# Four engines in written order across the hand-over between two stages, and low parts moved to GpSimd, in a gated attention and feed-forward kernel

## The chip, the cores and the metric

The kernel runs on one core of a Trainium2 chip. A core has a matrix engine (TensorE, PE in the profile), whose weight loads are listed apart (PEld), a vector engine (VectorE, DVE), a scalar engine (ScalarE, ACT), a general engine (GpSimd, POOL) and a queue that issues transfers (SyncE, SP). Each works through its own list of instructions in the order in which the list was built, and waits for the others through semaphores. The metric is the time of one execution on the device in microseconds (us); less is better.

## The reference, cut to what matters

```python
x = A_x                                            # 2048 tokens x 576, float32
g = sigmoid((x * gate_w).sum(-1, keepdims=True))   # one gate for each token
# A: linear attention, 32 heads of 18
q, k, v = heads(x @ wqkv)
pq, pk = q @ w_phi, k @ w_phi                      # by head
phi_q = [softmax(pq), softmax(-pq)]                # 36 features, phi_k likewise
kv, z = phi_k^T v, sum of phi_k over the tokens
a = (phi_q kv) / (phi_q z + 1e-6) @ wo
# B: feed-forward, 576 -> 4608 -> 576
gate, up = x @ W_gate, x @ W_up
b = (relu(gate) * up) @ W_down
out = g * a + (1 - g) * b
```

## The kernel before, in words

All products are to have float32 accuracy. An operand is split into a high part in the matrix engine's reduced format and a low part, the rest: ScalarE rounds a copy (the high part), another engine subtracts it from the source (the low part), and a product takes three passes: high by high, high by low, low by high. Every operand that enters a product therefore costs a copy on ScalarE and a subtraction, and the matmul waits for whichever part comes last.

**Attention, first half (to about 260 us).** Tokens are taken in 16 tiles of 128, four tiles to a block of 512. `load_x` loads a block's tokens (two transfers into tiles `xr` of the 4-buffer pool `raw`) and splits them into `xh`, `xl` and `x4`; `x4` holds the last 64 rows' high part and, in its other half, their low part. Block 0 is made ahead of the loop; the loop `for t in range(2, NT - 2)` makes block 1 at t = 3, block 2 at t = 6 and block 3 at t = 10. In a step t the matrix engine projects keys (`pk`), values (`kv`) and queries (`pq`) of a tile from `xh`, `xl`, `x4`, adds to the sums over keys (`kv<-e,vt`) and turns features (`ptr<-ident,e`). VectorE finds maxima and minima, subtracts them, sums the exponentials (`sm`) and scales one half of the features; GpSimd scales the others (L209, `e<-e,sm` for a key tile, `e<-e,r` for a query tile). PE, DVE and ACT are ordered here by the scheduler, GpSimd alone by `in_order`.

**Attention, second half.** The queries stand in four blocks of 512, b = 0 to 3. `sums(b, ..)` multiplies features by `kv`; `invert` and `split_inverse` make the reciprocals `rd`; `divide(b, k)` spreads `rd` over a bank (PE, L624), multiplies it into `R` (DVE, L626), copies the high part `oh` (ACT, L627) and subtracts the low part `ol` (DVE, L628). `project_out(b, m)` multiplies the five pieces k by `wo` for the output rows m, into one bank out of four (pool `pv1`, called `pw`, and `kv_bank(0..2)`, called `kv`), each of them one buffer: for b = 2, m = 0, 2, 4 take `pw` and m = 1, 3 take `kv2`; for b = 3, m = 0 to 4 take `kv1`, `pw`, `kv2`, `kv0`, `kv1`. So (2,4) may start when the copy of (2,2) has left `pw`, and (3,1) when (2,4) has left it. `rows_out` takes a bank out: for m < 4 one copy by ACT (L780), for m = 4 a copy by ACT (L782) and an addition by DVE that reads the bank too (L783).

**Hand-over to the feed-forward part.** Its products combine blocks of weights and of tokens (seven products `cx`, `ca`, `cy` in place of eight, L1122). Needed for the first of them are seven combined token operands `xo` and weights `wb` and `ws` for the first two groups of columns. Operands 0 to 2 are loaded ahead into `xr` and split by `operand_ahead`, a generator: its first step is the high part (ACT, L811), its second the low part (DVE, L815 and L825). Operands 3 to 6 are loaded in place and split by `in_place` (ACT L840 and L841, DVE L845 and L825). `first_weights` is a generator of steps: high parts of `wb` (ACT, L858), low parts (DVE, L861 and L864), four block sums in the raw weights `wr` (DVE, L879 to L882), and the same split for `ws`, which reads the sums. It also calls `in_place`.

From the end of the first half on, `in_order(tc, nc, nc.tensor, nc.sync, nc.gpsimd)` ties PE, SP and GpSimd to the order in which the code is written. ACT and DVE are not tied: the scheduler picks for them, except that `behind()` keeps the pieces of operands and weights behind the last instruction written before them and behind each other. A piece inside `behind()` may thus come much later than where it is written, behind the copies and divisions that are written after it. The names `first_out`, `root_rows`, `fetch` and `gather` are other steps of the attention part and stay as they are.

After this comes the feed-forward part, which is most of the time: `cx`, `ca`, `cy` products, ACT copies `g` and `u` out of their banks (L1288), DVE combinations (L1407 to L1412), and the down projection.

Of the kernel before, what the change touches and what calls it, by code (L numbers as in the profile page):

```python
# [7 lines left out]
F32 = mybir.dt.float32  # L8
# [7 lines left out]
P = 128  # L16
# [67 lines left out]
def gated_mix_kernel(  # L84
# [59 lines left out]
    wv_l = ka.tile([P, 5, VP], F32R, name="wv_l")  # L144
    bd = raw.tile([FG, NF, FG], F32, name="bd", tag="raw")

    def split(hi, lo, src):
        nc.scalar.activation(hi, src, AF.Copy)
        tt(out=lo, in0=src, in1=hi.bitcast(F32), op=SUB)

    X = {}

# [2 lines left out]
                 xp.tile([P, TB], F32R, name="x4"))  # L155
        return X[tb]

    def split_x4(x4, src):
        nc.scalar.activation(x4, src, AF.Copy)
        tt(out=x4[64:], in0=src[64:], in1=x4[64:].bitcast(F32), op=SUB)  # L160
# [12 lines left out]
    def accumulate(ps, pairs):  # L173
        for i, (w, m) in enumerate(pairs):
# [122 lines left out]
    def whole(steps):  # L297
        for _ in steps:
            pass
# [604 lines left out]
    def low_parts(f, u):  # L904
        f(u, low_w)
        f(u, low_w_rows)

    def first_weights():
        with behind():
            blocks(0, high_w)  # L910
            low_parts(blocks, 0)
            sums_of_blocks(0)
        yield
        with behind():
            blocks(1, high_w)
# [12 lines left out]
        yield  # L928
        for i in range(4, 7):
            in_place(i)  # L930
            yield
# [19 lines left out]
            load_operand(0, 2, nc.gpsimd)  # L951

    def in_place(i):
        with behind():
            high_in_place(0, i)
            low_in_place(0, i)
            low_rest(0, i, tt)

    with in_order(tc, nc, nc.tensor, nc.sync, nc.gpsimd):
        x0, x1, x2 = (operand_ahead(i) for i in range(3))  # L960
# [24 lines left out]
        for m in range(5):  # L985
            project_out(1, m)
            if m < 3:
                two = pp.tile([P, 2, TB], F32, name="po", tag="pp")
                sums(3, ORDER[2 * m:2 * m + 2], (two[:, 0], two[:, 1]))
            if m == 2:  # L990
                gather(3, 4)
            if m > 0:
                for k in ((), (4,), (3,), (2, 1), (0,))[m]:
                    divide(2, k)
            if m in (0, 1):
                root_rows(m + 2)
            if m == 2:
                with after(tc, nc, nc.vector, last_of(nc, nc.vector)):
                    invert(3)
                gather(3, 3, 2, 1, 0)  # L1000
                whole(split_inverse(3))
                whole(x0)
        for m in range(5):
            project_out(2, m)
            if m == 0:
                divide(3, 4)
                divide(3, 3)
                whole(x1)
            if m == 1:
                weights = first_weights()  # L1010
                for k in (2, 1, 0):
                    divide(3, k)
                RS.close()
                pad = ctx.enter_context(tc.tile_pool(name="pad2", bufs=1, **R_))
                pad.tile([P, 24], F32, name="pad2")
                xo2 = ctx.enter_context(tc.tile_pool(name="xo2", bufs=4, **R_))
                wop = ctx.enter_context(tc.tile_pool(name="wop", bufs=2, **R_))
                wraw = ctx.enter_context(tc.tile_pool(name="wraw", bufs=2, **R_))
                load_w(0)
                load_in_place(0, 3)  # L1020
                load_rests(0, (3, 4, 5))
                load_w(1)
                for i in range(4, 7):
                    load_in_place(0, i)
                whole(x2)
                load_rests(0, (6,))
                load_down(0)
                next(weights)
            if m > 1:
                next(weights)  # L1030
        load_w(2)
        for m in range(5):
            project_out(3, m)
            if m < 3:
                next(weights)
    AP.close()
    BS.close()

# [588 lines left out]
```

## Time and profile before

| what | value |
| --- | --- |
| three runs | 1592.48, 1590.77, 1590.91 us; median 1590.91 us |
| profiled execution | 1590.56 us |
| its span in the trace | 1588.8 us |
| PE busy | 1570.9 us (99% of the span) |
| DVE busy | 1190.6 us (75%) |
| ACT busy | 559.1 us (35%) |
| POOL busy | 175.0 us (11%) |
| mean granted TensorE clock | 0.999 |

The profile is one execution. A row of the timeline reads: start in us, duration in us, engine, line of the kernel, operation, output <- inputs with their shape, count of merged instructions, and in brackets the engine's idle time just before it with the instruction that ended it. Rows of waits read: waiting engine and line <- engine and line that released it: total us, number of times, longest us. Rows of windows read: stretch in us, its length, then busy us and count for PE, PEld, DVE, ACT, POOL, then the granted clock of PE as a fraction of full speed, the DMA engines' busy share and GB/s. The times are from the start of the span. Tile names have lost their numbers in these rows: `pw`, `kv` stand for the banks, `o` for the output rows, `R`, `oh`, `ol` for pieces of the divisions.

### The profile page before, as it was taken

How to read it: one execution, taken by the hardware profiler on the slowest of the kernel's cores; microseconds unless marked ns; L12 is line 12 of the kernel's file. 1: busy time of each engine (PE TensorE's matmuls, PEld its weight loads, DVE VectorE, ACT ScalarE, POOL GpSimd, SP SyncE). 2: the span in 40 equal slices, each digit the busy share in tenths (PEclk: the TensorE clock that was granted, in tenths of full speed). 3: DMA queues.
4: the chain of work that ended last, by engine and by line, in shares of the span. 5: the costliest groups of instructions: out<-in, count | busy, mean ns of one | idle time of the engine just before them, and what ended most of it. 6: DMA issues, size and time to landing. Idle time of an engine off the chain costs nothing.

```text
span 1588.8 us, 20172 instructions
## 1 busy us (share of the span) xinstructions
PE 1570.9 (99%) x7823; PEld 1312.6 (83%) x7823; DVE 1190.6 (75%) x1865; ACT 559.1 (35%) x918; POOL 175.0 (11%) x243
## 2 busy tenths in 40 slices
PE   9999999999999999999999999999999999999998
PEld 9999995577888888888888888888888888888887
DVE  4997775577778877787777777777777777777777
ACT  4444335553323333332333234232233232222321
POOL 0125521110000000000000002111111111111110
PEclk9999999999999999999999999999999999999999
DMA  5365415587655576555554516543343343443432
GB/s 171 108 205 182 154 41 158 162 331 283 217 213 210 215 257 221 215 198 216 198 195 179 208 77 229 193 172 148 140 180 146 143 177 131 167 168 131 179 140 75
DMA packets 64539, 283.38 MB, mean 178 GB/s; under 512 B 6802, under 2 KB 17298, under 8 KB 55740
## 3 DMA queue, kind: packets, MB, share of 16 engines
q1 hardware_dynamic: 61228, 270.34, 46.8%
q0 software_dynamic: 2352, 10.11, 2.0%
q10 hardware_dynamic: 864, 1.65, 0.3%
q8 instruction: 61, 1.00, 0.3%
q14 instruction: 34, 0.28, 0.0%
HBM read 172.07 MB, written 108.60 MB: 177 GB/s over the span
## 4 chain that ended last, share of the span: by engine, by line
PE 94%; DVE 4%; ACT 1%; DMA 0%; issue 0%; POOL 0%; SPq 0%; ACTq 0%; DVEq 0%; POOLq 0%
PE cx L1122 29%; PE ca L1122 14%; PE pd L1162 12%; PE pd L1185 10%; PE cy L1122 7%; PE kv L175 4%; PE pk L175 3%; PE pq L175 3%; PE pm L1162 2%; PE pm L1185 2%; PE kv L416 1%; PE ptr L374 1%; PE po L556 1%; PE pv L237 1%; PE pw L175 1%; PE psf L259 1%
## 5 line engine op out<-in xcount | busy, mean ns | idle before, releaser
L1227 ACT ACTIVATE hh<-g 128x512 fp32r<-128x512 f32 x195 | 119.9, 624 | 457.2 <-DVE g L1284 287.8
L1200 DVE TENSOR_TENSOR ac<-pd,ac 128x512 f32<-128x512 f32 x238 | 163.9, 689 | 144.4 <-PE pd L1185 144.2
L1122 PE MATMUL cx<-xo,ws 128*128 128x512 f32 x1008 | 253.5, 391 | 3.3 <-ACT g L1288 3.3
L1122 PE MATMUL ca<-xo,ws 128*128 128x512 f32 x1008 | 251.9, 389 | 0.0
L1122 PE MATMUL cx<-xo,wb 128*128 128x512 f32 x1008 | 249.1, 389 | 1.5 <-DVE u L1409 1.5
L1122 PEld LDWEIGHTS cx<-xo,ws 128*128 128x128 f32 x1008 | 190.0, 189 | 43.2 <-ACT g L1288 3.7
L1122 PEld LDWEIGHTS cx<-xo,wb 128*128 128x128 f32 x1008 | 188.1, 188 | 42.5 <-DVE u L1409 1.9
L1122 PEld LDWEIGHTS ca<-xo,ws 128*128 128x128 f32 x1008 | 189.2, 188 | 39.3
L1162 PE MATMUL pd<-hh,wd 128*128 128x512 f32 x576 | 200.7, 389 | 0.0
L1185 PE MATMUL pd<-hh,wd 128*128 128x512 f32 x476 | 185.2, 389 | 0.0
L1168 DVE TENSOR_TENSOR ac<-pd,ac 128x512 f32<-128x512 f32 x144 | 99.0, 688 | 105.3 <-PE pd L1162 102.5
L1232 DVE TENSOR_TENSOR hl<-g,hh 128x512 fp32r<-128x512 f32 x195 | 135.3, 694 | 1.9 <-ACT hh L1227 0.2
L1288 ACT ACTIVATE g<-cx 128x512 f32<-128x512 f32 x144 | 84.7, 588 | 130.1 <-PE cx L1122 130.0
L1162 PEld LDWEIGHTS pd<-hh,wd 128*128 128x128 f32 x576 | 108.1, 188 | 22.6
L1122 PE MATMUL cy<-xo,wb 128*128 128x512 f32 x504 | 126.0, 389 | 0.0
L1085 ACT ACTIVATE wd<-wdr 128x384 fp32r<-128x384 f32 (+1 forms) x106 | 62.3, 607 | 144.5 <-DMA wdr<-wd 144.5
L1162 PE MATMUL pd<-hl,wd 128*128 128x512 f32 x288 | 112.0, 389 | 0.0
L1122 PEld LDWEIGHTS cy<-xo,wb 128*128 128x128 f32 x504 | 94.8, 188 | 19.8
L1185 PEld LDWEIGHTS pd<-hh,wd 128*128 128x128 f32 x476 | 89.4, 188 | 18.5
L1185 PE MATMUL pd<-hl,wd 128*128 128x512 f32 x238 | 92.6, 389 | 0.0
L825 POOL TENSOR_TENSOR xo<-xr,xo 32x512 fp32r<-32x512 f32 x5 | 8.3, 1668 | 614.6 <-ACT xo L841 614.6
L1088 DVE TENSOR_TENSOR wd<-wdr,wd 128x384 fp32r<-128x384 f32 (+1 forms) x106 | 68.8, 663 | 2.0 <-ACT wd L1085 2.0
(256 smaller groups left out, 2559.8 us busy)
## 6 DMA issues: line engine op xcount, KB each, us to landing
wsd<-ws SPq DMA_DIRECT2D x34, 1280.0 KB
ws<-wsd SPq DMA_DIRECT2D x34, 1280.0 KB
wbd<-wb SPq DMA_DIRECT2D x34, 960.0 KB
wb<-wbd SPq DMA_DIRECT2D x34, 960.0 KB
wr<-wgu SPq DMA_DIRECT2D x36, 768.0 KB
wdr<-wd SPq DMA_DIRECT2D x36, 576.0 KB
eT<-et SPq DMA_DIRECT2D x10, 594.0 KB
xt<-xb SPq DMA_DIRECT2D x7, 768.0 KB
```

Source lines behind the costliest of these rows:

```text
L175: nc.tensor.matmul(ps, w, m, start=i == 0, stop=i == len(pairs) - 1)
L237: nc.tensor.matmul(pv[i][c], m, w_[:, k, cs], start=k == 0 and n == 0, stop=k == 4 and n == 1)
L1085: nc.scalar.activation(o[:, 0], a, AF.Copy)
L1088: tt(out=o[:, 1], in0=a, in1=o[:, 0].bitcast(F32), op=SUB)
L1122: nc.tensor.matmul(ps, w, v, start=first and m == 0, stop=m == len(pairs) - 1, skip_group_check=True)
L1162: nc.tensor.matmul(ps, w, v, start=k == 0 and (i < 2 or first), stop=k == len(mms) - 1 and (i < 2 or last), skip_group_check=True)
L1168: tt(out=a, in0=ps, in1=a, op=ADD)
L1185: mm = lambda ps, w, v, a, z: nc.tensor.matmul(ps, w, v, start=a, stop=z, skip_group_check=True)
L1200: tt(out=a, in0=ps, in1=a, op=ADD)
L1227: nc.scalar.activation(h, src, AF.Copy)
L1232: tt(out=l, in0=src, in1=h.bitcast(F32), op=SUB)
L1288: nc.scalar.activation(a, ps, AF.Copy)
```

## The change

Three things are done.

First, block 1's tokens. `load_x` becomes a generator that issues both loads and then, in a second step, splits. For block 1 the loads are issued at t = 2 and the split is written at t = 3 as before, with `pt`, GpSimd's subtraction, in place of DVE's. With it the first three pieces are copied and subtracted one at a time (128x512 each) instead of as one 128x1536 instruction.

Second, operand 0's split (`x0`) is written after the step m = 4 of the loop over `project_out(1, m)`, behind the divisions of block 2, where it stood at m = 2.

Third, the hand-over. From `project_out(2, 1)` on, `in_order` holds all engines, DVE and ACT included, and `behind()` is taken out of `first_weights` and `in_place`. The transfers are written as `load_w(0)`, `load_w(1)`, the four in-place loads, three of the rests, `load_down(0)`; operand 2's split and the last rest move into `first_weights`, into its third step; `load_w(2)` moves behind the last `project_out`.

```diff
-    def load_x(tb):
+    def load_x(tb, f=tt):
         s = slice(tb * TB, (tb + 1) * TB)
         xh, xl, x4 = x_tiles(tb)
-        a = raw.tile([P, 3, TB], F32, name="xr", tag="raw")
+        a, b = (raw.tile([P, n, TB], F32, name="xr", tag="raw") for n in (3, 2))
         nc.sync.dma_start(a, xT[:, 0:3, s])
-        split(xh[:, 0:3], xl[:, 0:3], a)
-        b = raw.tile([P, 2, TB], F32, name="xr", tag="raw")
         nc.sync.dma_start(b, xT[:, 3:5, s])
-        split(xh[:, 3], xl[:, 3], b[:, 0])
-        split_x4(x4, b[:, 1])
+        yield
+        for k in (slice(0, 3),) if f is tt else range(3):
+            split(xh[:, k], xl[:, k], a[:, k], f)
+        split(xh[:, 3], xl[:, 3], b[:, 0], f)
+        split_x4(x4, b[:, 1], f)
...
-            if t in (3, 6, 10):
-                load_x((t + 2) // 4)
+            if t == 2:
+                second = load_x(1, pt)
+                next(second)
+            if t == 3:
+                whole(second)
+            if t in (6, 10):
+                whole(load_x(t // 4 + 1))
...
     def first_weights():
-        with behind():
-            blocks(0, high_w)
-            low_parts(blocks, 0)
-            sums_of_blocks(0)
+        blocks(0, high_w)
+        low_parts(blocks, 0)
+        sums_of_blocks(0)
         yield
-        with behind():
-            blocks(1, high_w)
-            low_parts(blocks, 1)
+        blocks(1, high_w)
+        low_parts(blocks, 1)
         yield
-        with behind():
-            block_sums(0, high_w)
-            sums_of_blocks(1)
-        with behind():
-            block_sums(1, high_w)
-            low_parts(block_sums, 0)
+        block_sums(0, high_w)
+        whole(x2)
+        load_rests(0, (6,))
+        sums_of_blocks(1)
+        yield
+        low_parts(block_sums, 0)
+        block_sums(1, high_w)
         yield
         in_place(3)
-        with behind():
-            low_parts(block_sums, 1)
+        low_parts(block_sums, 1)
         yield
...
                 whole(split_inverse(3))
+            if m == 4:
                 whole(x0)
-        for m in range(5):
+        project_out(2, 0)
+        divide(3, 4)
+        divide(3, 3)
+        whole(x1)
+    with in_order(tc, nc, nc.tensor, nc.vector, nc.scalar, nc.gpsimd, nc.sync):
+        project_out(2, 1)
+        for k in (2, 1, 0):
+            divide(3, k)
...
+        load_w(0)
+        load_w(1)
+        for i in range(3, 7):
+            load_in_place(0, i)
+        load_rests(0, (3, 4, 5))
+        load_down(0)
+        weights = first_weights()
+        next(weights)
+        for m in range(2, 5):
             project_out(2, m)
...
+            next(weights)
         for m in range(5):
             project_out(3, m)
-            if m < 3:
-                next(weights)
+            next(weights, None)
+        load_w(2)
```

What this does to the lists of instructions is seen at three places. In the rows, a name's number tells tiles of the same name apart.

GpSimd in step t = 3 of the first half, before (`e_600` is the first query tile's feature scaling, `e_673` the next key tile's):

```order
L209 TENSOR_TENSOR e_499<-e_499,sm_503 128x32x18
L209 TENSOR_TENSOR e_556<-e_556,sm_560 128x32x18
L209 TENSOR_TENSOR e_600<-e_600,r_606 128x32x18
L209 TENSOR_TENSOR e_673<-e_673,sm_677 128x32x18
L209 TENSOR_TENSOR e_717<-e_717,r_723 128x32x18
```

And after (`e_607` and `e_677` are those two, `xl_524` and `x4_525` block 1's low parts):

```order
L210 TENSOR_TENSOR e_499<-e_499,sm_503 128x32x18
L210 TENSOR_TENSOR e_563<-e_563,sm_567 128x32x18
L210 TENSOR_TENSOR e_607<-e_607,r_613 128x32x18
L149 TENSOR_TENSOR xl_524<-xr_526,xh_523 128x512 x3
L149 TENSOR_TENSOR xl_524<-xr_527,xh_523 128x512
L160 TENSOR_TENSOR x4_525<-xr_527,x4_525 64x512
L210 TENSOR_TENSOR e_677<-e_677,sm_681 128x32x18
```

Five subtractions now stand behind the first query tile's scaling and ahead of the next key tile's. The matmuls on tile 4, the first of block 1, wait for them one by one.

ACT from the copy of (2,1) on, before (`o_3511<-pw_3496` is the copy of (2,2), `o_3533` of (2,3), `o_3556` of (2,4), `o_3583` of (3,0)):

```order
L780 ACTIVATE o_3427<-kv2_3412 128x512
L627 ACTIVATE oh_3396<-R_3223 128x512 x2
L780 ACTIVATE o_3511<-pw_3496 128x512
L627 ACTIVATE oh_3396<-R_3223 128x512
L811 ACTIVATE xo_3480<-xr_3329 128x1536
L780 ACTIVATE o_3533<-kv2_3518 128x512
L782 ACTIVATE o_3556<-pw_3546 64x512
L858 ACTIVATE wb_3488<-wr_3464 128x3x384
L780 ACTIVATE o_3583<-kv1_3568 128x512
L780 ACTIVATE o_3605<-pw_3590 128x512
L858 ACTIVATE wb_3514<-wr_3472 128x3x384
```

And after (`o_3509` is the copy of (2,2), `o_3531` of (2,3), `o_3556` of (2,4), `o_3579` of (3,0)):

```order
L786 ACTIVATE o_3431<-kv2_3416 128x512
L633 ACTIVATE oh_3400<-R_3227 128x512 x3
L864 ACTIVATE wb_3486<-wr_3468 128x3x384
L786 ACTIVATE o_3509<-pw_3494 128x512
L864 ACTIVATE wb_3512<-wr_3470 128x3x384
L786 ACTIVATE o_3531<-kv2_3516 128x512
L864 ACTIVATE ws_3534<-wr_3468 128x4x384
L817 ACTIVATE xo_3536<-xr_3380 128x1536
L788 ACTIVATE o_3556<-pw_3546 64x512
L864 ACTIVATE ws_3562<-wr_3470 128x4x384
L786 ACTIVATE o_3579<-kv1_3564 128x512
```

The copy of (2,2) has gone behind all three divisions' `oh` and the first `wb`; that of (2,4) behind both `wb`, the first `ws` and operand 2.

DVE from the last three divisions on, before (`o_3556<-o_3556,pw_3546` is the addition that frees the bank of (2,4)):

```order
L626 TENSOR_TENSOR R_3223<-kv1_3430,R_3223 128x512
L626 TENSOR_TENSOR R_3223<-kv0_3435,R_3223 128x512
L626 TENSOR_TENSOR R_3223<-pr_3440,R_3223 128x512
L628 TENSOR_TENSOR ol_3397<-R_3223,oh_3396 128x512 x3
L815 TENSOR_TENSOR xo_3480<-xr_3329,xo_3480 128x1024
L825 TENSOR_TENSOR xo_3480<-xr_3329,xo_3480 32x512
L783 TENSOR_TENSOR o_3556<-o_3556,pw_3546 64x512
L861 TENSOR_TENSOR wb_3488<-wr_3464,wb_3488 128x3x256
```

And after, from the second group's `wb` on; ahead of these rows stand the third division's `ol`, the first group's two `wb` rows and its four sums:

```order
L867 TENSOR_TENSOR wb_3512<-wr_3470,wb_3512 128x3x256
L870 TENSOR_TENSOR wb_3512<-wr_3470,wb_3512 32x3x128
L821 TENSOR_TENSOR xo_3536<-xr_3380,xo_3536 128x1024
L831 TENSOR_TENSOR xo_3536<-xr_3380,xo_3536 32x512
L885 TENSOR_TENSOR wr_3470<-wr_3470 128x384
L886 TENSOR_TENSOR wr_3470<-wr_3470 128x384
L887 TENSOR_TENSOR wr_3470<-wr_3470 128x384
L888 TENSOR_TENSOR wr_3470<-wr_3470 128x384
L789 TENSOR_TENSOR o_3556<-o_3556,pw_3546 64x512
L867 TENSOR_TENSOR ws_3534<-wr_3468,ws_3534 128x4x256
```

The addition `o_3556` now has fourteen instructions between the last `ol` and itself, where it had two. The three divisions, whose `R` stood together, now alternate with their `ol`. The matmuls of `project_out` and of the products stand on PE in the same order as before.

More of the change, by code (lines that the diff above doesn't have):

```diff
@@ L145, in gated_mix_kernel, with split @@
     bd = raw.tile([FG, NF, FG], F32, name="bd", tag="raw")
-    def split(hi, lo, src):
+    def split(hi, lo, src, f=tt):
         nc.scalar.activation(hi, src, AF.Copy)
-        tt(out=lo, in0=src, in1=hi.bitcast(F32), op=SUB)
+        f(out=lo, in0=src, in1=hi.bitcast(F32), op=SUB)
     X = {}
@@ L156, in x_tiles, with split_x4 @@
         return X[tb]
-    def split_x4(x4, src):
+    def split_x4(x4, src, f=tt):
         nc.scalar.activation(x4, src, AF.Copy)
-        tt(out=x4[64:], in0=src[64:], in1=x4[64:].bitcast(F32), op=SUB)
-    def load_x(tb):
+        f(out=x4[64:], in0=src[64:], in1=x4[64:].bitcast(F32), op=SUB)
+    def load_x(tb, f=tt):
         s = slice(tb * TB, (tb + 1) * TB)
         xh, xl, x4 = x_tiles(tb)
-        a = raw.tile([P, 3, TB], F32, name="xr", tag="raw")
+        a, b = (raw.tile([P, n, TB], F32, name="xr", tag="raw") for n in (3, 2))
         nc.sync.dma_start(a, xT[:, 0:3, s])
-        split(xh[:, 0:3], xl[:, 0:3], a)
-        b = raw.tile([P, 2, TB], F32, name="xr", tag="raw")
         nc.sync.dma_start(b, xT[:, 3:5, s])
-        split(xh[:, 3], xl[:, 3], b[:, 0])
-        split_x4(x4, b[:, 1])
+        yield
[3 more added lines that the diff above has]
+        split_x4(x4, b[:, 1], f)
     def accumulate(ps, pairs):
@@ L953, in in_place @@
     def in_place(i):
[L954 to L957, printed above, removed]
+        high_in_place(0, i)
+        low_in_place(0, i)
+        low_rest(0, i, tt)
     with in_order(tc, nc, nc.tensor, nc.sync, nc.gpsimd):
@@ L1001, in gated_mix_kernel @@
                 whole(split_inverse(3))
+            if m == 4:
                 whole(x0)
-        for m in range(5):
-            project_out(2, m)
[L1005 to L1027, printed above, removed]
-                next(weights)
-            if m > 1:
-                next(weights)
-        load_w(2)
+        project_out(2, 0)
[6 more added lines that the diff above has]
+            divide(3, k)
+        RS.close()
+        pad = ctx.enter_context(tc.tile_pool(name="pad2", bufs=1, **R_))
+        pad.tile([P, 24], F32, name="pad2")
+        xo2 = ctx.enter_context(tc.tile_pool(name="xo2", bufs=4, **R_))
+        wop = ctx.enter_context(tc.tile_pool(name="wop", bufs=2, **R_))
+        wraw = ctx.enter_context(tc.tile_pool(name="wraw", bufs=2, **R_))
+        load_w(0)
[7 more added lines that the diff above has]
+        for m in range(2, 5):
+            project_out(2, m)
+            next(weights)
         for m in range(5):
             project_out(3, m)
-            if m < 3:
-                next(weights)
+            next(weights, None)
+        load_w(2)
     AP.close()
```

## Prediction

> **What bounds the kernel.** I read the page first, then the waits of PE, then windows to place them, then the timeline of the two places that the change touches.
>
> ```profile
> span 1588.8 us, 20172 instructions
> PE 1570.9 (99%) x7823; PEld 1312.6 (83%) x7823; DVE 1190.6 (75%) x1865; ACT 559.1 (35%) x918; POOL 175.0 (11%) x243
> ```
>
> PE is idle for 17.9 us in all. Beyond that and the clock no rearrangement can win anything, and whatever keeps PE waiting anywhere is lost unless a later wait of PE swallows it. The waits and the windows show where the idle time is:
>
> ```profile
> PE cx L1122 <- ACT g L1288: 3.3, 1, 3.3
> PE cx L1122 <- DVE u L1409: 1.5, 1, 1.5
> PE ptr L374 <- POOL e L209: 1.2, 2, 0.7
> ```
>
> ```profile
> 60.00:80.00 20.00, 18.83 (x151) 17.69 (x148) 18.18 (x28) 8.36 (x13) 3.96 (x3) 1.00 0.36 118
> 80.00:230.00 150.00, 150.00 (x1258) 144.61 (x1257) 121.22 (x186) 62.02 (x98) 62.42 (x40) 1.00 0.42 148
> 340.00:350.00 10.00, 6.73 (x29) 5.30 (x28) 9.12 (x11) 9.52 (x13) 0.54 (x1) 0.96 0.75 251
> 350.00:360.00 10.00, 10.00 (x40) 8.09 (x39) 8.01 (x12) 2.66 (x5) 0.55 (x1) 0.87 1.00 420
> ...
> 370.00:380.00 10.00, 9.80 (x43) 8.09 (x44) 6.90 (x12) 4.04 (x6) 0.00 (x0) 1.00 1.00 324
> 380.00:1500.00 1120.00, 1120.00 (x4942) 926.27 (x4941) 850.07 (x1327) 362.37 (x593) 75.39 (x145) 1.00 0.50 185
> ```
>
> In the third number of a window PE is busy 150.00 of 150 between 80 and 230 us and 1120.00 of 1120 after 380: PE alone sets the pace there, so a microsecond that it loses before 80 or before 380 arrives at the end whole. The largest wait, 3.3 us, is at the hand-over near 347, where ACT is 95% busy.
>
> **The change, early part.** VectorE loses three subtractions and GpSimd gains five.
>
> ```profile
> 58.70 1.74 DVE L149 TENSOR_TENSOR xl<-xr,xh 128x1536 fp32r<-128x1536 f32 x1
> 60.63 0.62 DVE L149 TENSOR_TENSOR xl<-xr,xh 128x512 fp32r<-128x512 f32 x1
> 61.17 0.17 DVE L358 TENSOR_TENSOR r<-r,sm 128x32 f32<-128x32 f32 x1
> 61.37 0.69 DVE L160 TENSOR_TENSOR x<-xr,x 64x512 fp32r<-64x512 f32 x1
> 62.09 0.76 DVE L194 TENSOR_REDUCE mx<-pk 128x32 f32<-128x576 f32 x1
> ...
> 61.48 1.60 POOL L209 TENSOR_TENSOR e<-e,r 128x576 f32<-128x576 f32 x1 [5.32 <-DVE r L358]
> ...
> 59.77 0.76 PE L416 MATMUL kv<-e,vt 128*55 128x108 f32 x10
> 63.15 0.65 PE L374 MATMUL ptr<-ident,e 128*108 128x128 f32 x4 [0.69 <-POOL e L209]
> ```
>
> and, for one line each, shortest, median and longest duration in ns with first and last start:
>
> ```profile
> L825 POOL TENSOR_TENSOR xo<-xr,xo x5: 1279/1282/2264, 963.1 to 974.9; 32x512 fp32r<-32x512 f32 x5
> L209 POOL TENSOR_TENSOR e<-e,r x14: 1167/1172/1604, 61.5 to 235.0; 128x576 f32<-128x576 f32 x14
> ```
>
> No row shows a 128x512 subtraction on POOL. The nearest is L825's, the same operation into the same type with the same 512 elements per partition: 1.28 us (the duration goes by elements per partition, if 32 and 128 partitions count alike). Cheaper end: L209 scaled from 576 to 512 elements, 1.17 x 512/576 = 1.04. Dearer end: L209 when VectorE runs beside it, 1.60; L825's longest, 2.26, is one of five. I take 1.28.
>
> In the old trace block 1's low parts were there by 62.06, and PE worked on them from 60.49 while POOL still scaled the query tile. Now they start only behind that scaling. VectorE reaches `r` earlier, since 2.36 us of subtractions stand no longer ahead of it, but two reductions of the next key tile (0.76 for the first) slip in and ACT's five separate copies cost it a little: `r` at about 60.9, scaling until 62.2. The five then end near 63.5, 64.8, 66.0, 67.3 and 68.6. PE's list has eleven `kv<-e,vt` (done near 61.0), then the turn `ptr` (waits until 62.2: 1.2 us), one value matmul on the first low part (0.8), and key matmuls on the other four (0.15, 0.85, 0.85, 1.15), because between two of these waits stand only one to nine matmuls of about 0.12 us (18.83 us for 151 of them in the window from 60 to 80). That is 5.0 us of idle. The 1.17 us of the old trace (the two waits for POOL `e`) go, the second since VectorE now runs ahead. Net +3.8; if PE arrives a little later at `ptr`, as my reading of its place is no better than 0.9 us, +2.9. I take **+3.4**. With 1.04 for each it is 1.2 less (+2.2), with 1.60 it is 1.6 more (+5.0). The cover that used to hide the subtractions (value matmuls) is now written behind the waits, so nothing hides them.
>
> The Trainium skill ("SBUF — State Buffer", Who interferes with whom) says that a VectorE instruction with two SBUF inputs and a GpSimd instruction that reads SBUF lock each other out. L209 on POOL at 1.17 against 1.60 fits, and by it alone the five would take up to 1.6 us more whenever VectorE runs such instructions beside them; in that stretch most of VectorE's inputs come from PSUM, so I leave it to the range.
>
> The other block-1 edits cost nothing visible: issuing block 1's transfer earlier can only bring it earlier, and the output-weight load that gives way to it feeds work that ACT and VectorE do between 60 and 80 us, where ACT is busy 8.4 of 20 us.
>
> **Operand 0 moved.** Around 306 to 315 VectorE made operand 0's low part ahead of the first divisions, and PE waited three times:
>
> ```profile
> 310.07 0.50 PE L624 MATMUL kv<-rd,spread 128*128 128x512 f32 x1 [0.86 <-DVE R L626]
> 313.72 0.51 PE L175 MATMUL pw<-oh,wo 128*128 128x512 f32 x1 [0.44 <-ACT oh L627]
> 314.84 0.49 PE L175 MATMUL pw<-ol,wo 128*128 128x512 f32 x1 [0.61 <-DVE ol L628]
> ```
>
> 1.91 us. The subtraction goes behind them; what is late next is the inverse from POOL, for which PE then waits about 0.8. I take **-1.2** (bounds -1.9 and 0). It only helps PE: VectorE has the same work until operand 1 is done, at 321.1.
>
> **The hand-over.** The old rows, in that trace's times:
>
> ```profile
> 321.14 1.29 DVE L626 TENSOR_TENSOR R<-kv,R 128x512 f32<-128x512 f32 x2
> 322.94 2.07 DVE L628 TENSOR_TENSOR ol<-R,oh 128x512 fp32r<-128x512 f32 x3
> 325.69 1.23 DVE L815 TENSOR_TENSOR xo<-xr,xo 128x1024 fp32r<-128x1024 f32 x1 [0.68 <-ACT xo L811]
> ...
> 328.96 0.68 DVE L783 TENSOR_TENSOR o<-o,pw 64x512 f32<-64x512 f32 x1 [1.34 <-ACT o L782]
> 330.01 0.96 DVE L861 TENSOR_TENSOR wb<-wr,wb 128x768 fp32r<-128x768 f32 x1 [0.38 <-ACT wb L858]
> 330.98 0.55 DVE L864 TENSOR_TENSOR wb<-wr,wb 32x384 fp32r<-32x384 f32 x1
> 331.57 0.56 DVE L879 TENSOR_TENSOR wr<-wr 128x384 f32<-128x384 f32 x1
> ...
> 323.17 0.60 ACT L780 ACTIVATE o<-pw 128x512 f32<-128x512 f32 x1
> 323.66 0.63 ACT L627 ACTIVATE oh<-R 128x512 fp32r<-128x512 f32 x1
> ...
> 328.83 1.15 ACT L858 ACTIVATE wb<-wr 128x1152 fp32r<-128x1152 f32 x1
> 336.27 1.48 ACT L858 ACTIVATE ws<-wr 128x1536 fp32r<-128x1536 f32 x1
> ...
> 326.09 0.62 PE L175 MATMUL pw<-oh,wo 128*128 128x512 f32 x2
> 328.13 0.84 PE L175 MATMUL kv<-oh,wo 128*128 128x512 f32 x3
> 331.30 0.84 PE L175 MATMUL pw<-oh,wo 128*128 128x512 f32 x3
> 342.86 1.75 PE L1122 MATMUL cx<-xo,wb 128*128 128x512 f32 x7
> 349.47 3.35 PE L1122 MATMUL cx<-xo,ws 128*128 128x512 f32 x7 [3.27 <-ACT g L1288]
> ```
>
> Before, PE never waited between 320 and 343: the copy of (2,2) came at 323.17 and the addition of (2,4) at 328.96, each long before its bank was wanted. Now both stand in a row with the splits.
>
> First stall, (2,4) for the copy of (2,2). From 321.1 the three divisions go R (0.69), `oh` on ACT (0.63), `ol` (0.69) in turn: R, oh, ol, R, oh, ol, R, oh make 8 pieces, 5.4 us, so the last `oh` ends at 326.5. ACT then makes the first `wb` (1.15, to 327.6) and only then copies (2,2), to 328.1. PE would want the bank at 326.09 - 1.2 = 324.9: **3.2 us**.
>
> Second stall, (3,1) for the addition of (2,4). VectorE: first `wb` low 0.96 + 0.55 from 327.6 to 329.1; four sums of 0.56, to 331.4; second `wb` low to 332.9, meanwhile ACT makes the first `ws` from the sums (1.48, to 332.9) and operand 2's high part (the same shape, to 334.3). Operand 2's low part 1.23 + 0.69 (its third piece has 512 elements, as R), to 336.2; four sums, to 338.4; the addition, to 339.0. PE, having started (2,4) at 328.1, ends it at 330.2 and (3,0) 3.2 later, at 333.4: **5.6 us**. Of the new order nothing hides these; transfers are not late (`wr` is there long before in either order).
>
> From there (3,1) to (3,4) take 11.6 (331.30 to 342.86): the first `cx` starts at 339.0 + 11.6 = 350.6, that is 7.7 later than 342.86 (-1.2 + 3.2 + 5.6). In return ACT has done the in-place operands between the copies and takes out the first bank at once: the wait of 3.27 goes (bound: at least 2 of it), **-3.3**. The 1.5 us wait at `u` hangs on work that stays in its order and remains. What is late next at the hand-over is nothing that I can find.
>
> **The clock.** Behind the 3.27 us wait seven matmuls took 3.35 us where the seven at 342.86 took 1.75, and the windows granted 0.96 and 0.87: 0.4 + 1.3 = 1.7 us lost, as half speed for 3.4 us would make it. With the wait gone this goes, but a 5.6 us wait is longer than the one that brought it, so I take it as coming back once: net 0. The wait of 1.5 us, at 370.2, brought none (the window from 370 was granted 1.00). Whether the 3.2 us one does is open: 0 or +1.7.
>
> The Trainium skill ("TensorE: Matmul & The Clock Gate", What's actually happening) lets the clock fall after an idle window of about 3.4 us that runs freely against the kernel. By it a 5.6 us wait need not, though it probably does, cover such a window, and a 3.2 us one would not; that would give the sum as it stands, or 1.7 less. The old trace, where 3.27 us sufficed, is a shade more severe than the rule.
>
> **Sum** against the profiled 1590.56 (the median of the runs is 0.35 higher): +3.4 - 1.2 + 3.2 + 5.6 - 3.3 + 0 = +7.7, so **1598.3 us**.
>
> **Rivals.**
> 1. *Half speed behind both new stalls* (or POOL's five at 1.60): +1.7, 1600.0; both together, 1601.6. For it: 3.2 is next to 3.27. Against: the 3.27 may have been a matter of phase.
> 2. *Half speed behind neither:* -1.7, 1596.6. Against it: 5.6 us is 1.7 times the wait that sufficed.
> 3. *Faster.* One mechanism: the divisions' chain starts earlier, because without operand 0 ahead of it VectorE runs operand 1's split and R sooner than 321.1, and both banks come free in time. Then -3.3 at `g`, -1.7 of clock, -1.2 at operand 0 stand against +3.4: -2.8, 1587.8. It decides where the two stalls together fall under 2.8 us. Against it: the second stall is made of 11.2 us of VectorE and ACT work between 327.2 and 338.4 against 8.5 us that PE has from 324.9 to 333.4, so even a first stall of zero leaves some 5.
> 4. *About the same.* The early part costs +1.3 (low parts at 1.04, PE 0.9 later), the second stall shrinks to 2 and brings no half speed: 1.3 - 1.2 + 3.2 + 2.0 - 3.3 - 1.7 = +0.3, 1590.9. It wants several misjudgements at once.
>
> A lesser uncertainty is whether the early loss is swallowed by the small waits between 230 and 320; these hang on chains that PE itself feeds, so I give it no term.
>
> **How the numbers follow.** Forecast with one half-speed stretch 0.45 (its own range 1596 to 1600.5), rival 1 0.20, rival 2 0.20, rival 4 0.07, rival 3 0.08. The range runs from 1594.0 (rival 2 with the early part at +2.2 and some of the second stall lost) to 1602.0 (rival 1 at its upper end); it leaves out rivals 3 and 4 and a little above. A measurement of this kernel can tell about 0.2%, 3.2 us, from no change: faster 0.07, same 0.09 (rival 4 and the edges of 2 and 3), slower 0.84.
>
> **What would show it.** On PE: waits for POOL `xl` between 62 and 69 that sum to 3 us or more, and PE full from 80 to 230 as before; a wait near 328 (plus the early shift) with ACT's copy of `pw` as releaser, some 3 us; one near 337 with VectorE's addition (L789) as releaser, 5 to 6 us, and half speed behind it; no wait of `cx` for `g`. If the L789 wait is under 2 us, or the POOL waits under 1, I am wrong in that term, and if both are, in the sign.

## The result: slower by 0.6%, and the profile after

The changed kernel takes 1600.32 us (median of six executions, 1596.90 to 1603.17) against 1590.92 for the kernel before: a ratio of 1.0059, 95% interval 1.0045 to 1.0073. The forecast was 1598.3, in a range from 1594.0 to 1602.0. The profiled execution is the quickest of the six, 1596.90 us with a span of 1595.1, so the profile shows +6.3 of the median's +9.4; where the rest comes from is the first of the experiments.

The waits of PE in the changed kernel (waiting line <- releasing line: total us, times, longest):

```profile
PE pw L176 <- ACT o L786: 3.0, 1, 3.0
PE pw L176 <- DVE o L789: 2.9, 1, 2.9
PE cx L1122 <- DVE u L1409: 1.5, 1, 1.5
...
PE pk L176 <- POOL xl L149: 1.1, 2, 0.6
PE kv L417 <- DVE e L210: 1.1, 1, 1.1
PE pk L176 <- POOL x L160: 0.9, 1, 0.9
PE ptr L375 <- POOL e L210: 0.7, 1, 0.7
PE kv L176 <- POOL xl L149: 0.6, 1, 0.6
```

The wait of `cx` for `g`, 3.3 us before, is gone. Two waits for the bank `pw` and five small ones in the first half have come. The timeline shows what released each:

```profile
61.71 1.17 POOL L210 TENSOR_TENSOR e<-e,r 128x576 f32<-128x576 f32 x1 [4.38 <-DVE r L359]
62.83 5.00 POOL L149 TENSOR_TENSOR xl<-xr,xh 128x512 fp32r<-128x512 f32 x4
67.91 1.26 POOL L160 TENSOR_TENSOR x<-xr,x 64x512 fp32r<-64x512 f32 x1
...
330.60 0.58 ACT L786 ACTIVATE o<-pw 128x512 f32<-128x512 f32 x1
...
341.76 0.67 DVE L789 TENSOR_TENSOR o<-o,pw 64x512 f32<-64x512 f32 x1
...
243.79 0.65 PE L375 MATMUL ptr<-ident,e 128*108 128x128 f32 x4 [0.36 <-ACT ph L384]
331.23 1.22 PE L176 MATMUL pw<-oh,wo 128*128 128x512 f32 x2 [3.04 <-ACT o L786]
342.48 0.96 PE L176 MATMUL pw<-oh,wo 128*128 128x512 f32 x3 [2.95 <-DVE o L789]
354.18 1.75 PE L1122 MATMUL cx<-xo,wb 128*128 128x512 f32 x7
357.35 1.75 PE L1122 MATMUL cx<-xo,ws 128*128 128x512 f32 x7
```

```profile
60.00:70.00 10.00, 6.64 (x55) 5.17 (x53) 8.86 (x14) 2.28 (x3) 8.13 (x7) 1.00 0.37 115
80.00:230.00 150.00, 149.71 (x1257) 144.30 (x1256) 120.54 (x182) 62.46 (x98) 61.01 (x40) 1.00 0.43 148
...
330.00:340.00 10.00, 8.30 (x23) 6.29 (x23) 7.93 (x12) 6.17 (x7) 1.09 (x2) 0.66 0.80 308
340.00:350.00 10.00, 7.52 (x33) 6.25 (x34) 9.07 (x12) 6.41 (x9) 1.67 (x3) 1.00 0.62 164
```

Set beside the old trace, PE's lateness can be followed. The row of that trace that the prediction does not show is

```profile
239.75 0.65 PE L374 MATMUL ptr<-ident,e 128*108 128x128 f32 x4 [0.36 <-ACT ph L383]
```

The turn `ptr` that ends the first half starts at 243.79, and stood at 239.75: +4.0. (2,4) is wanted at 331.23 - 3.04 = 328.2, and started at 326.09: +2.1, so 1.9 came back in between, where operand 0 was moved. (3,1) starts at 342.48 in place of 331.30: +11.2. The third product starts at 357.35 in place of 349.47: +7.9, since 3.3 us of waiting for `g` are gone. The old trace then lost 1.6 us to half speed at that place (3.35 us for seven matmuls) and the new one does not: +6.3, and there it stays to the end.

The window from 330 to 340 has a granted clock of 0.66, and two matmuls of (2,4) take 1.22 us where they took 0.62: half speed for 6.8 us, 3.4 us lost, behind the first wait. It cost nothing here. (3,1) waits for VectorE's addition at 341.76, and PE's slowness only shortened that wait, to 2.95 where the forecast had 5.6.

### The profile page after: what moved, and what is told of

Read it like the earlier page. It is cut to its first block, busy times and chain, and to the rows that moved or that the text cites. A ratio compares the mean times of both kernels' runs of the same rounds, so it can differ in the third digit from the quotient of the medians.

```text
span 1595.1 us, 20181 instructions
## 1 busy us (share of the span) xinstructions
PE 1572.7 (99%) x7823; PEld 1314.0 (82%) x7823; DVE 1189.9 (75%) x1862; ACT 559.9 (35%) x920; POOL 181.3 (11%) x248
## 4 chain that ended last, share of the span: by engine, by line
PE 94%; DVE 3%; DMA 1%; ACT 1%; issue 1%; POOL 0%; SPq 0%; DVEq 0%; POOLq 0%; ACTq 0%
PE cx L1122 28%; PE ca L1122 14%; PE pd L1162 12%; PE pd L1185 10%; PE cy L1122 7%; PE kv L176 4%; PE pq L176 3%; PE pk L176 3%; PE pm L1162 2%; PE pm L1185 2%; PE kv L417 1%; PE po L562 1%; PE ptr L375 1%; PE pv L238 1%; PE pw L176 1%; PE psf L260 1%
## 5 line engine op out<-in xcount | busy, mean ns | idle before, releaser
L864 ACT ACTIVATE ws<-wr 128x1536 fp32r<-128x1536 f32 x36 | 53.7, 1491 | 50.5 <-DVE wr L888 50.5
```

The source lines that it names most:

```text
L864: nc.scalar.activation(o[:, :, 0:3], a, AF.Copy)
```

## The experiments

All are compared with the kernel before in executions on the same chip; intervals are 95%.

### The changed kernel once more

> The changed kernel once more, to see what differs between its executions (1596.9 to 1603.2 us, where the kernel before has 1589.9 to 1592.5). Theory: the times fall into steps of what half-speed stretches of PE cost. In the profile of the quickest execution the clock fell behind the wait for the copy of (2,2), for 3.4 us worth, but that loss lay inside the second wait (2.95 us left of it); where it falls behind the second wait, nothing hides it and the time is 1.7 to 3.4 us more. So 1597 to 1601 here, with the two waits for the bank together at 5.5 to 9 us and the stretch of low clock at another place whenever the time is longer. Rival: the spread comes from the early part or from transfers; then another profile shows a PE wait of some us that the first one does not have, ahead of 300 us or on a DMA.

1600.05 us (median of five, 1596.90 to 1604.02), ratio 1.0056, 1.0042 to 1.0070. This profile is of an execution of 1599.73:

```profile
PE pw L176 <- DVE o L789: 4.1, 1, 4.1
PE pw L176 <- ACT o L786: 3.0, 1, 3.0
...
PE kv L417 <- DVE e L210: 1.4, 1, 1.4
```

```profile
60.00:70.00 10.00, 6.66 (x54) 5.19 (x54) 8.86 (x14) 2.28 (x3) 8.08 (x7) 1.00 0.37 116
70.00:80.00 10.00, 10.00 (x66) 10.00 (x65) 6.76 (x10) 4.37 (x7) 2.05 (x2) 0.83 0.31 106
...
330.00:340.00 10.00, 7.13 (x23) 5.38 (x23) 7.28 (x11) 7.17 (x8) 1.09 (x2) 0.83 0.93 372
340.00:350.00 10.00, 6.01 (x20) 4.89 (x21) 9.06 (x13) 4.64 (x6) 1.21 (x3) 0.83 0.46 111
```

Three stretches of half speed, each of which loses 0.17 x 10 = 1.7 us. The middle one lies ahead of the second wait, which covers it. The last lies behind it and counts, as expected. The first I had not expected: it stands at 70 to 80, behind the small waits of the early part, and counts too. So the theory (steps of half speed) holds and the rival is half right: one of the steps comes from the early part. The 2.8 us between the two profiled executions are near the 3.4 that these two stretches cost: (3,1) starts 1.5 later than in the first profile (343.99), the third product 2.9 later (360.22).

### The parts alone

```diff
 early_only:     the kernel before with the changed load_x and loop over t
 handover_only:  the kernel before with the rest of the change
 x0_only:
+            if m == 4:
                 whole(x0)
```

> Only block 1's part of the change (loads at t = 2, five subtractions on GpSimd); the rest as before. Theory: +4.0 us (the last feature turn of the first half moved from 239.75 to 243.79 us between the two profiles), all of it passed on: 1594.9, within 1 us from execution to execution, and PE waits for POOL xl and x of 2.5 us or more. The wait at g of 3.27 us stays. Rival (the loss is absorbed by the small waits from 230 to 320 or by the wait at g): 1591 to 1592. Rival (this part makes the spread): times that differ by 4 us or more.

1596.00 us, ratio 1.0030 (1.0021 to 1.0039). The eleven executions lie in three heaps: five at 1594.6 to 1594.9, four at 1596.0 to 1597.1, two at 1598.9 to 1599.0. The quickest heap is the +4.0 of the theory, so the loss is passed on whole. The profiled execution is one of the slowest heap. Its trace has one stretch of half speed from 70 to 80, with a granted clock of 0.83 (1.7 us), and 2.2 us that PE lost at the very start, ahead of everything that was edited:

```profile
9.37 0.45 PE L238 MATMUL pv<-wv_l,xh 128*128 128x294 f32 x1
...
11.29 0.30 PE L238 MATMUL pv<-wv_l,xh 128*128 128x294 f32 x1
...
23.81 2.27 PE L260 MATMUL psf<-bd,wr 126*128 126x126 f32 x18
```

In the kernel before's trace the last of these rows stands at 21.58. That this part also makes a spread was the second rival's point, and I had expected 1 us at most: it holds for the 1.7, not for the 2.2 of the start. For the middle heap there is only the mean clock.

> Only the second and third part (operand 0 behind the divisions, all engines in written order from (2,1) on); block 1 as before. Theory: 1590.9 + 2.2 = 1593.1 where half speed falls into the second wait, up to 1596.5 where it falls behind it, so a spread of 3 us or more here; two PE waits for the bank pw at (2,4) and (3,1). Rival (the hand-over costs nothing, the loss is all early): 1590 to 1591. Rival (the order takes the clock loss and the wait at g away and the stalls are an effect of the early lateness): faster than 1589.

1595.40 us (1592.82 to 1596.85), ratio 1.0024 (1.0014 to 1.0035), with waits of 3.0 and 4.3 for the bank. So the hand-over loses by itself, as the theory had it; both rivals fall. By the medians, 5.16 from the one part and 4.56 from the other make 9.7, the change as a whole costs 9.2 to 9.4: the parts add up.

> Only the second part: operand 0's split is written at m = 4 instead of m = 2, nothing else. Theory: the three waits of PE at 310 to 315 us shrink from 1.91 to about 0.4, but PE then arrives earlier at the wait for g, which hangs on ACT's row of splits, and waits longer there: 3.3 becomes 4 to 5 us, the time stays within 1 us of 1590.9, or it loses some more to half speed as the wait is longer. Rival: ACT and VectorE come earlier as well and the 1.5 us show in the time: 1589.4.

1590.26 us, ratio 0.9994 (0.9986 to 1.0003), no difference that this can tell. In its trace the gain is eaten where the theory said:

```profile
PE cx L1123 <- ACT g L1289: 4.0, 1, 4.0
```

```profile
340.69 1.75 PE L1123 MATMUL cx<-xo,wb 128*128 128x512 f32 x7
...
348.02 3.36 PE L1123 MATMUL cx<-xo,ws 128*128 128x512 f32 x7 [4.00 <-ACT g L1289]
351.18 2.87 PE L1123 MATMUL cy<-xo,wb 128*128 128x512 f32 x7
```

PE comes to the products 2.2 earlier and waits 4.0 instead of 3.3 for `g`. The larger part goes to half speed behind that wait: the seven matmuls of `cy` take 2.87 where they took 1.80, and 0.3 us of the gain are left.

### What in the early part costs

> The kernel before with block 1's loads at t = 2 (and their place in the queue), but with the three subtractions left on VectorE. In the early-only run's trace PE waited 1.0 us for VectorE's key scaling near 57, which it did not do before, and ACT made a key tile's exponentials 1.4 us later (46.01 against 44.59) since block 1's five copies now stood ahead of them. Theory (the loss of 4 us has two parts, 1 us of ACT's order and 3 us of GpSimd): 1592.0, with the wait near 57 there and no wait for xl. Rival (all of it is GpSimd's five subtractions): 1590.8 and no new wait. Rival (all of it is ACT's order): 1595.

Against early_only:

```diff
-                second = load_x(1, pt)
+                second = load_x(1)
```

1592.47 us, ratio 1.0006 (0.9997 to 1.0014): the loss is 1.4 by the medians, which the interval does not separate from zero. The wait is there in the trace:

```profile
48.12 1.15 ACT L202 ACTIVATE e<-e 128x1152 f32<-128x1152 f32 x1
...
53.86 0.92 PE L417 MATMUL kv<-e,vt 128*55 128x108 f32 x14 [1.22 <-DVE e L210]
```

This wait ends at 53.9 here, and at 51.8 in the changed kernel. The exponentials stand at 48.12, but this execution too lost 2.2 us at the start (its first matmuls of L260 stand at 23.77). The changed kernel's first profile, which lost none there, shows the delay itself, and the 46.01 of the expectation is its figure and not that of early_only. Before, and then after:

```profile
39.94 0.73 ACT L438 ACTIVATE woo<-wor 128x640 fp32r<-128x640 f32 x1
...
44.59 1.17 ACT L201 ACTIVATE e<-e 128x1152 f32<-128x1152 f32 x1 [2.47 <-DVE e L200]
```

```profile
44.62 0.62 ACT L159 ACTIVATE x<-xr 128x512 fp32r<-128x512 f32 x1
45.37 0.74 ACT L439 ACTIVATE woo<-wor 128x640 fp32r<-128x640 f32 x1
46.01 1.15 ACT L202 ACTIVATE e<-e 128x1152 f32<-128x1152 f32 x1
```

The exponentials come 1.4 later. Block 1's copies now stand ahead of them, and so does the copy of the output weights `woo`, whose load gave way to block 1's.

> The kernel before with block 1's five subtractions on GpSimd and the copies by pieces, but the loads left at t = 3. Theory: the four to five waits for xl and x stay (0.6 to 0.9 each, 2.7 in all, and 0.7 for the turn), the wait near 57 does not come: +2.5 to +3 without half speed, 1593.5 to 1594, some executions 1.7 more where the low clock follows on waits that sum to 3 us within 6. Rival (all of it is ACT's order): 1590.8.

Against early_only:

```diff
-            if t == 2:
-                second = load_x(1, pt)
-                next(second)
             if t == 3:
-                whole(second)
+                whole(load_x(1, pt))
```

1595.46 us (1593.52 to 1597.73), ratio 1.0022 (1.0012 to 1.0032). The four waits are in the trace, and the one for `e` is not:

```profile
PE pk L176 <- POOL xl L149: 1.2, 2, 0.6
PE pk L176 <- POOL x L160: 0.9, 1, 0.9
...
PE ptr L375 <- POOL e L210: 0.7, 1, 0.7
...
PE kv L176 <- POOL xl L149: 0.6, 1, 0.6
```

The size is 1.5 above what I expected. Two of the nine executions stand at 1597.5 to 1597.7 with a mean clock of 0.996, the quickest two at 1593.5 to 1593.7 with 0.999, so half speed is again the likely reason for most of that; the profiled execution, at 1594.3, does not show it. GpSimd's subtractions, with the copies by pieces that go with them here, are the larger of the two causes. The early loads, which put copies ahead of exponentials on ACT, are the smaller, and for them only the wait is shown, not a time.

### What in the hand-over costs

> The hand-over part with project_out(2,2) written ahead of the last two divisions, so that ACT copies it before it waits for them. Theory: the first wait (3.0) goes to zero and nothing is won, because (3,1) starts when VectorE's row reaches the addition, wherever PE stands: the second wait grows by what the first one gave, to 7 to 9 us, and the time stays near 1595.4, or 1 to 2 lower or higher with the number of half-speed stretches that remain. Rival (each wait costs its own length): 1595.4 - 3.0 - 1.7 of clock = 1590.7.

Against handover_only:

```diff
-        for k in (2, 1, 0):
-            divide(3, k)
+        divide(3, 2)
+        project_out(2, 2)
+        divide(3, 1)
+        divide(3, 0)
...
-        for m in range(2, 5):
+        next(weights)
+        for m in range(3, 5):
```

1595.67 us (1595.08 to 1596.88), ratio 1.0025 (1.0016 to 1.0034), the time of the hand-over as it was.

The start of (3,1) in handover_only, and then here:

```profile
338.45 1.65 PE L175 MATMUL pw<-oh,wo 128*128 128x512 f32 x3 [4.29 <-DVE o L783]
```

```profile
338.57 1.65 PE L175 MATMUL pw<-oh,wo 128*128 128x512 f32 x3 [9.09 <-DVE o L783]
```

One wait of 9.1 us stands in place of 3.0 and 4.3, and (3,1) starts at the same time. The first wait was worth nothing by itself: VectorE's row sets when (3,1) starts. The rival, by which each wait costs its length, is out by 5 us.

> The hand-over part with project_out(2,3) and (2,4) written ahead of operand 2's split and the second group's sums, so that the addition that frees the bank of (2,4) stands six instructions earlier on VectorE. Theory: the second wait (4.3) goes; the first (3.0) stays. The splits that stood ahead of it now stand behind it, so ACT comes to the copy g later against PE and 1 to 3 us of the wait at g come back. 1595.4 - 4.3 + 2 = 1593, less 1.7 if one half-speed stretch goes with it: 1591 to 1593. Rival (VectorE and ACT have the same work to do before the first products, so it only changes place): 1595, with the 4.3 us back at g. Rival (the wait goes and nothing comes back): 1589.5.

Against handover_only:

```diff
-        for m in range(2, 5):
-            project_out(2, m)
-            next(weights)
+        project_out(2, 2)
+        next(weights)
+        project_out(2, 3)
+        project_out(2, 4)
+        next(weights)
+        next(weights)
```

1589.71 us (1588.65 to 1593.46), ratio 0.9990 (0.9981 to 0.9999), better than expected by 1.3 at least and level with the kernel before or a little quicker. Its timeline:

```profile
327.72 1.11 PE L175 MATMUL pw<-oh,wo 128*128 128x512 f32 x2 [3.05 <-ACT o L780]
346.21 1.75 PE L1119 MATMUL cx<-xo,wb 128*128 128x512 f32 x7
...
350.15 1.88 PE L1119 MATMUL cx<-xo,ws 128*128 128x512 f32 x7 [0.61 <-ACT g L1285]
```

The second wait is gone, and of the wait at `g` only 0.6 came back: close to the rival by which nothing comes back. Nor is there half speed behind that wait, where the kernel before lost 1.6 us. Where the addition stands in VectorE's row was the cause of the hand-over's loss.

> The hand-over part with both moves: project_out(2,2) ahead of the last two divisions, and (2,3) and (2,4) ahead of operand 2's split and the second group's sums. Theory: with the addition out of the row, the first wait is no longer covered by a later one, so taking it away counts now; but ACT's and VectorE's splits are the same work, so ACT comes to g about 3 us later against PE: the wait at g is 3 to 4 us with half speed behind it, as in the kernel before. 1589.7 - 3.0 + 3.0 = 1589.7, and up to 1591.5 with the clock. Rival (the first wait comes out whole): 1586.7.

The edit is the two diffs above together.

1588.92 us, ratio 0.9986 (0.9977 to 0.9996), 0.8 below the range that I gave and 2.2 above the rival.

```profile
334.68 1.65 PE L175 MATMUL pw<-oh,wo 128*128 128x512 f32 x3 [3.39 <-DVE o L783]
```

The first wait is gone, the one at `g` too, but PE waits 3.4 us at (3,1) for the addition, which still stands behind the first group's sums and the second group's `wb`. I had put the wait at `g`; that three microseconds remain is right, the place is not.

> Both moves, and the second group's sums and its split of ws taken out from ahead of the first products: its sums are written behind the last project_out, its ws is split during the first unit of products; operands 3 to 6 come ahead of them. The output is the same. Theory (what bounds the hand-over is the row of splits on VectorE and ACT ahead of g): no wait for the bank pw, the wait at g goes as well, a wait at u of 1.5 to 2 us stays, no half speed: 1590.9 - 3.3 - 1.7 - 1.2 + 0.5 = 1585.2. Rival (the splits only change place): the time goes back into waits at u and g in the first three units, 1589 to 1591.

The divisions are written as in handover_copy_first; the rest of the edit is

```diff
-        weights = first_weights()
...
+        blocks(0, high_w)
+        low_parts(blocks, 0)
+        project_out(2, 3)
+        project_out(2, 4)
+        sums_of_blocks(0)
+        whole(x2)
+        load_rests(0, (6,))
+        block_sums(0, high_w)
+        low_parts(block_sums, 0)
+        project_out(3, 0)
+        in_place(3)
+        blocks(1, high_w)
+        low_parts(blocks, 1)
+        project_out(3, 1)
+        for i in range(4, 7):
+            in_place(i)
+            project_out(3, i - 2)
+        sums_of_blocks(1)
...
+        if u == 0 and j == 4:
+            low_parts(block_sums, 1)
...
-            if make:
+            if make or u == 0:
                 block_sums(v, high_w)
```

1588.73 us, ratio 0.9986 (0.9977 to 0.9995). The first `cx` starts at 340.8, 2.1 earlier than before the change, without a wait for the bank or for `g`. But:

```profile
340.78 1.75 PE L1105 MATMUL cx<-xo,wb 128*128 128x512 f32 x7
...
353.53 6.28 PE L1105 MATMUL cx<-xo,wb 128*128 128x512 f32 x14 [3.07 <-DVE u L1394]
```

VectorE comes to `u` 3.1 us late, and fourteen matmuls behind that wait take 6.28 where they take 3.5 at full speed. The theory's 1585.2 is missed by 3.5; the rival, 1589 to 1591 with the time back in such waits, was near.

> As second_group_later, with the second group's ws copied by ACT behind the first down weights and split by VectorE behind the first unit's last gating, so that its 1.9 us stand no longer ahead of u. In the trace of second_group_later VectorE reached u 3.1 us late, by ACT's copy of ws (it waited 1.56 us for it) and this split, and PE ran at half speed behind the wait. Theory: the wait at u of the first unit goes, with its half speed (3.1 + 3.4), one of 1.5 to 1.9 us at the second unit stays: 1584 to 1585, all executions within 2 us. Rival (the split is only late again one unit on): 1588.

Against second_group_later:

```diff
-        if u == 0 and j == 4:
-            low_parts(block_sums, 1)
...
             gated(a, T["u2"])
+            if u == 0:
+                low_parts(block_sums, 1)
...
-            if make or u == 0:
+            if make:
                 block_sums(v, high_w)
...
                 plain_down(0, (high, low)[j - 3])
+                if j == 3:
+                    block_sums(1, high_w)
```

1586.65 us (1584.70 to 1588.06), ratio 0.9971 (0.9959 to 0.9982): quicker than both kernels, though the median is above the 1584 to 1585 that I expected and the spread is 3.4 where I had 2. The profiled execution took 1584.86:

```profile
PE cx L1105 <- DVE u L1392: 2.1, 1, 2.1
```

```profile
330.00:340.00 10.00, 10.00 (x46) 8.28 (x45) 9.70 (x13) 8.74 (x12) 1.65 (x3) 1.00 0.92 285
...
360.00:370.00 10.00, 7.94 (x36) 6.23 (x34) 7.25 (x10) 4.37 (x6) 0.00 (x0) 1.00 1.01 420
```

PE is full from 320 to 350 and the clock was granted 1.00 throughout, behind the 2.1 us wait too. Other executions, at 1586.7 and 1588.1 with a mean clock of 0.999 and 0.998, are above it by 1.8 and 3.2, about one and two such stretches.

## Why the prediction was right, and where its sizes were off

The sign, the two places and the releasers came as forecast, and the median lay in the range; two of its six executions lay above it. That the median comes to 2.0 us from the forecast is in part luck, since some terms that were off make up for others. By its own terms:

- **Early part, +3.4:** +4.0 in the profiled execution. GpSimd's five subtractions took 1.25 each (5.00 for four, 1.26) where I took 1.28, and ended at 69.2 where I had 68.6. What I undersized is ACT: I let its five copies "cost it a little", and the new order cost PE a wait of 1.1 to 1.4 us near 52, since exponentials queued behind them. The output weights that I placed between 60 and 80 are part of it: their first copy on ACT stood at 39.94 and now stands at 45.37, right ahead of those exponentials. The waits for GpSimd, 0.57 to 0.95 each, sum to 3.4 where I had 5.0, and those for `xl` and `x` alone to 2.7, under the 3 that I had named as the sign. So the one error hides most of the other.
- **SBUF rule:** the Trainium skill's lock ("SBUF — State Buffer", Who interferes with whom) would have stretched the five where VectorE runs an instruction with two SBUF inputs beside them. In that stretch it ran one (L210, 1.42 us, beside the last of the five), and the five took 1.25 to 1.26 each, so they show nothing of it.
- **Operand 0, -1.2:** -1.9 on the way, at the edge of its bounds. Alone it is worth nothing that the run with it alone can tell, and in the whole it only lengthens the first stall.
- **First stall, 3.2:** 3.04. **Second, 5.6:** 2.95 and 4.12 in two executions. The row that I added up on VectorE was nearly right: (3,1) started 11.2 later, and the forecast has 3.4 + 7.7 = 11.1. But 4.0 of the 11.2 are the early part, so the row made 7.1 to 7.2 (7.15 in handover_only) in place of 7.7, and the two errors of 0.6 cancel. The wait is shorter since PE itself came late, at half speed: (2,4) and (3,0) took 8.3 and 7.1 us where I had 5.3, and without that the wait would have been about 6.0 in both. That the first stall is only a part of this row, and not a loss of its own, the sum had right, though its two terms stand there as if each counted; the run with the copy first shows it.
- **The wait at g, -3.3:** gone.
- **The clock, 0:** this is the term that was mis-sized. I took half speed as coming back once, behind the second stall. In the quickest execution it came behind the first and was hidden, so 1.6 us better; the median is 3.4 us above that execution. Part of this lies behind the second stall, as in rival 1, and part behind the early waits, of which none is over 1.4 us and to which I had given no clock at all. The profiles show this for two executions; of the others only the mean clock is known, 0.995 to 0.997, and whether they also lost time at the start, as three profiles of other runs did, is open.
- **Clock rule:** the Trainium skill's window of about 3.4 us ("TensorE: Matmul & The Clock Gate", What's actually happening) fits the length of the stretches, 1.7 us lost in one and 3.4 in two on end. By that section's idle window a 3.04 us wait, or PE 66% busy from 60 to 70, would not bring the clock down; a wait of 3.0 us did in the four profiles that have one, the other in one profile of the changed kernel and not in the other. The measurement decides.

## What to carry to other kernels

Ordering an engine by hand puts whatever frees a buffer in line with everything written ahead of it: before writing splits ahead of a copy or an addition that empties a bank, add up the row, and move the emptying instruction to the front. Of two waits in sequence, ask which one is the end of a row on another engine; taking away the other only moves its time. Where the matrix engine sets the pace, several waits of half a microsecond close together can, in some executions, cost more than their sum.

## What the runs showed of the hardware that I had not expected

The clock falls without a single long wait. In one execution PE was busy 6.66 of 10 us between 60 and 70, with no single wait over 1 us in that stretch, and ran at a granted 0.83 in the next ten; in another, with 6.64 of 10, it kept 1.00. early_only and early_subtract_gpsimd have the same waits, and their profiles differ in the same way: 0.83 in the first, 1.00 in the second. One wait of 3.0 us brought half speed for 6.8 us in one execution and for 3.4 in another, and a wait of 2.1 us brought none in the execution seen. What decides between these is not settled by these runs; that it differs between executions of one program would fit something that runs free of it, which is not shown.

Not all that differs is in the granted clock. In early_only a matmul of 128x294 takes 0.45 us until 10.8 and 0.30 after it, while the granted clock from 6 to 10 reads 1.00. The first L260 matmuls start at 23.8 there and in early_loads_vector, and at 23.4 in handover_both_first; in the other ten profiles (L259 or L260) they start between 21.4 and 22.0. These 2 us lie ahead of every edit, and handover_only, which begins as handover_both_first does, is not among the three. What brings them is open.

Executions of one kernel then stand on steps, the kernel before too: 1589.6, 1590.9 and 1592.6 are where most of its executions lie, at mean clocks of 1.000, 0.999 and 0.998 or 0.999. A single execution can be off by two such steps, so an interval needs several.
